# A long convolution in six channel parts inside the first feed-forward units, with the feed-forward width in thirds

## The chip, the cores and the metric

The kernel runs on one core of a Trainium2 chip. The metric is the time of one execution on the device in microseconds (us); less is better. A profile is one further execution, recorded by the hardware: it lists what each engine did and when. The engines are PE (matrix products), PEld (loads of its weights, which overlap them), DVE (vector operations), ACT (activations), POOL (a general vector engine that here also issues the loads of x) and SP, which here only issues transfers. Transfers run on 16 DMA engines.

## The reference

Two layers, each of a gated convolution (A) and a gated feed-forward (B), on x of 2048 tokens by 576 channels. The convolution has the same inputs k, v, ssm_k in both layers, so its y is the same in both.

```python
def _A_ref(q, k, v, shift_k, ssm_k, ssm_D):
    # k_shift: causal filter of 4 taps along the tokens
    kv = k_shift * v
    y = irfft(rfft(kv, 2S) * rfft(ssm_k, 2S))[:S]     # causal convolution of length S = 2048
    return q * (y + kv * ssm_D)

def _B_ref(x, w_gate, w_up, w_down):                  # 576 -> 4608 -> 576
    return (_gelu(x @ w_gate) * (x @ w_up)) @ w_down

x = A_q
for _ in range(2):
    x = x + _A_ref(_layernorm(x), ...)
    x = x + _B_ref(_layernorm(x), ...)
```

## The kernel before

**The convolution** (`ssm_conv`) works on four blocks of 512 tokens. A block of kv or of the filter h is turned into a spectrum of 1024 rows by matmuls with a matrix GF (`fwd`, L125 to L132: for each of 8 row tiles four matmuls, then ACT copies PSUM to SBUF). GF and the inverse matrix GI are made on the chip: DVE makes integer phases (L55, L59), ACT takes their sine (L60). For block m, DVE multiplies spectra K of block a with H of block m - a (L219), PE sums the products in PSUM by matmuls with an identity (L223), ACT copies the sum to Y (L229), DVE adds the Y of the block before with a sign, which makes Z (L233, L236), and PE brings it back with GI (L242), from where ACT copies it into y_sb (L244). The 576 channels go in two parts, of 512 and of 64. kv is made in eight groups of 256 tokens: four shifted loads of k and one of v, all double-buffered, then eight DVE operations (L178 to L183).

All of the convolution stands ahead of the feed-forward. Only the loads of x for chunk 0, its gate and its normalisation, and the first three weight groups are put in after block 0 (`on_block`, L390).

**The feed-forward** goes in eight units, a unit being one layer of one chunk of 512 tokens: (0,0), (0,1), (1,0), (0,2), (1,1), (0,3), (1,2), (1,3) as (layer, chunk). A unit has a gate/up phase and a down phase. In gate/up, for each of 36 tiles f of 128 features, 18 matmuls (L438) with K of 64 rows fill two PSUM banks, ACT applies the gelu to one (L441) and DVE multiplies by the other into hT (L442); four pairs of banks are used in turn. Weights of w_gate and w_up arrive in groups of three f (wgu, three buffers, L298 to L301, rows of 768 bytes). In the down phase, for each of four rows j of 128 tokens, 36 pairs of matmuls of 512 and 64 columns (L458, L459) sum over f; DVE adds x (L466, L467). w_down (wd) is loaded once, in unit 0, and stays (L430).

The next unit's gate (`gate_steps`: mean and variance, POOL's power for 1/sigma at L329, two DVE operations) and normalisation (`ln_steps`) are DVE steps that are taken one by one after each f (L443); then eight transposing transfers (`spread`, L358) make xnT, the moving operand of the next gate/up phase. These are issued after the gate/up phase, so that the down phase lies beside them. After layer 0's down phase the gate of layer 1 follows at once (L471).

A scheduler of the framework decides the order of instructions on each engine, by dependences and program order. Transfers issued by SP go out in SP's order.

Of the kernel before, what the change touches and what calls it, by code (L numbers as in the profile page):

```python
# [11 lines left out]
ALU = mybir.AluOpType  # L12
# [11 lines left out]
def _gen_dft_mats(tc, pool_gf, pool_gi, G_dtype):  # L24
    nc = tc.nc
    N4 = 4 * NDFT
    KT_F = BS // P
    KT_I = NDFT // P
    GF = pool_gf.tile([P, KT_F, NDFT], G_dtype, name="GF")
    GI = pool_gi.tile([P, KT_I, BS], G_dtype, name="GI")  # L30
    with ExitStack() as es:
        tmpc = es.enter_context(tc.tile_pool(name="dft_tmp", bufs=1))
        work = es.enter_context(tc.tile_pool(name="dft_work", bufs=2))
        rowv = tmpc.tile([P, KT_F], F32, name="rowv")
        nc.gpsimd.iota(rowv[:], pattern=[[2 * P, KT_F]], base=1, channel_multiplier=2,
                       allow_small_or_imprecise_dtypes=True)
        rowf = tmpc.tile([P, 2, KT_F], F32, name="rowf")
        nc.gpsimd.iota(rowf[:], pattern=[[0, 2], [2 * P, KT_F]], base=1, channel_multiplier=2,
                       allow_small_or_imprecise_dtypes=True)
        colf = tmpc.tile([P, NF], F32, name="colf")  # L40
        nc.gpsimd.iota(colf[:], pattern=[[2, NF]], base=1, channel_multiplier=0,
                       allow_small_or_imprecise_dtypes=True)
        colt = tmpc.tile([P, BS], F32, name="colt")
        nc.gpsimd.iota(colt[:], pattern=[[2, BS]], base=2, channel_multiplier=0,
                       allow_small_or_imprecise_dtypes=True)
        negpi = tmpc.tile([P, 1], F32, name="negpi")
        nc.vector.memset(negpi[:], -math.pi)
        sc = 2.0 * math.pi / N4

        def emit(dst, col_ap_halves, row_scalar, offs):  # L50
            W = sum(w for _, w in col_ap_halves)
            j = work.tile([P, NDFT], I32, tag="dft_j", bufs=1)
            c0 = 0
            for (cap, w), off in zip(col_ap_halves, offs):
                nc.vector.tensor_scalar(out=j[:, c0:c0 + w], in0=cap, scalar1=row_scalar,  # L55
                                        scalar2=float(off), op0=ALU.mult, op1=ALU.add)
                c0 += w
            jm = work.tile([P, NDFT], I32, tag="dft_jm")
            nc.vector.tensor_single_scalar(out=jm[:, 0:W], in_=j[:, 0:W], scalar=N4 - 1, op=ALU.bitwise_and)  # L59
            nc.scalar.activation(out=dst, in_=jm[:, 0:W], func=ACT.Sin, bias=negpi[:], scale=sc)  # L60

        for kt in range(KT_F):
            emit(GF[:, kt, :], [(colf[:], NF), (colf[:], NF)], rowv[:, kt:kt + 1],
                 [3 * NDFT, 0])
        for kt in range(KT_I):
            off = 3 * NDFT if kt < KT_F else 0
            emit(GI[:, kt, :], [(colt[:], BS)], rowf[:, kt // KT_F, kt % KT_F: kt % KT_F + 1], [off])
    return GF, GI

@with_exitstack
def ssm_conv(ctx, tc, y_sb, ident, A_k, A_v, A_shift_k, A_ssm_k, A_ssm_D, on_block):
    nc = tc.nc
    G_dtype = BF16
    k2 = A_k[0]
    v2 = A_v[0]
    S, D = k2.shape
    NST = S // P
    NBLK = S // BS  # L80
    STB = BS // P
    KT_F = BS // P
    KT_I = NDFT // P
    MT = NDFT // P
    HM = MT // 2
    KS = A_shift_k.shape[1]
    parts = []
    o = 0
    while o < D:
        w = min(512, D - o)  # L90
        parts.append((o, w))
        o += w

    fpool = ctx.enter_context(tc.tile_pool(name="A_freq", bufs=1))
    gip = ctx.enter_context(tc.tile_pool(name="A_gi", bufs=1))
    psT = ctx.enter_context(tc.tile_pool(name="A_psT", bufs=4, space=PSUM))
    psY = ctx.enter_context(tc.tile_pool(name="A_psY", bufs=2, space=PSUM))

    kv_es = ExitStack()
    gfp = kv_es.enter_context(tc.tile_pool(name="A_gf", bufs=1))  # L100
    kvp = kv_es.enter_context(tc.tile_pool(name="A_kv", bufs=2))
    dvec = gfp.tile([1, D], BF16, name="dvec")
    nc.sync.dma_start(out=dvec[:], in_=A_ssm_D.unsqueeze(0))

    def load_h(blk):
        hT = kvp.tile([P, STB, D], BF16, tag="blk", name=f"hT{blk}")
        nc.sync.dma_start_transpose(out=hT[:], in_=A_ssm_k[:, blk * BS:(blk + 1) * BS])
        return hT

    hT_next = load_h(0)  # L110
    GF, GI = _gen_dft_mats(tc, gfp, gip, G_dtype)
    kc = kv_es.enter_context(tc.tile_pool(name="A_kc", bufs=1))
    ktmp = kv_es.enter_context(tc.tile_pool(name="A_ktmp", bufs=2))
    sgn_i = gip.tile([P, 1], I32, name="sgn_i")
    nc.gpsimd.iota(sgn_i[:], pattern=[[0, 1]], base=0, channel_multiplier=1)
    sgn_b = gip.tile([P, 1], I32, name="sgn_b")
# [406 lines left out]
```

## Time and profile before

Three runs took 1095.11, 1095.13 and 1094.2 us: median 1095.11. The profiled execution took 1096.94 us, with a span of 1095.2 us from its first to its last instruction.

| engine | busy us | share of the span | instructions |
|---|---|---|---|
| PE | 1014.3 | 93% | 8433 |
| PEld | 488.2 | 45% | 8496 |
| DVE | 499.2 | 46% | 1024 |
| ACT | 256.3 | 23% | 486 |
| POOL | 56.8 | 5% | 79 |

The page moves 122.81 MB in all, 112 GB/s over the span. A share of busy time is a mean over stages that differ: one has to ask which stage has which limit, and which wait ends last there. PE's 93% also counts matmuls whose ends are modelled and which overlap, so it does not say how near PE is to its own limit; the start-to-start distances on PE's timeline do.

### The profile page before, as it was taken

Reading aid. Unit: us, or ns where it says so; the run is one execution under the profiler, and the core shown is the slowest. Engines: PE = TensorE matmul, PEld = TensorE weight load, DVE = VectorE, ACT = ScalarE, POOL = GpSimd, SP = SyncE. Lnnn points to the kernel's source line nnn. Section 1 sums busy time; section 2 is a strip of 40 time slices with the busy share of each in tenths; the row PEclk is TensorE's granted clock in tenths of the full one; section 3 lists DMA queues with packets and bytes.
Section 4 is the critical chain, followed back from the end, with each engine's and each line's share of the span. In section 5 each row is a group of like instructions: output and inputs, shape, how many; then the busy total and the mean of one; then the engine's idle time right before and its main releaser. Section 6 shows DMA issues by size and latency. Waiting matters only on the chain.

```text
span 1095.2 us, 19986 instructions
## 1 busy us (share of the span) xinstructions
PE 1014.3 (93%) x8433; PEld 488.2 (45%) x8496; DVE 499.2 (46%) x1024; ACT 256.3 (23%) x486; POOL 56.8 (5%) x79
## 2 busy tenths in 40 slices
PE   4887688869999999799999997999999999999998
PEld 1343233425554445355544453555444544454444
DVE  6396689673355323943123338432233553203320
ACT  5565232113202320133023201330132023202310
POOL 2000100020010001300000012000000100000000
PEclk9899889989999999999999999999999999999999
DMA  9881100297734772377457733674377347725710
GB/s 183 197 268 33 27 18 1 63 289 154 145 66 95 151 139 51 66 145 150 91 129 149 149 58 66 130 160 90 77 160 143 67 96 150 141 65 120 147 38 17
DMA packets 183802, 122.81 MB, mean 112 GB/s; under 512 B 54053, under 2 KB 181536, under 8 KB 183712
## 3 DMA queue, kind: packets, MB, share of 16 engines
q1 hardware_dynamic: 181600, 116.81, 51.3%
q0 software_dynamic: 2112, 4.72, 1.5%
q8 instruction: 66, 1.08, 0.4%
q14 instruction: 24, 0.20, 0.1%
HBM read 104.98 MB, written 2.36 MB: 98 GB/s over the span
## 4 chain that ended last, share of the span: by engine, by line
PE 79%; DVE 13%; issue 3%; DMA 2%; POOL 1%; ACT 1%; SPq 0%; DVEq 0%; POOLq 0%
PE ps L438 47%; PE ps L458 22%; PE ps L459 4%; PE ps L129 3%; DVE pr L219 3%; DVE stats L321 2%; PE ps L242 2%; PE Yps L223 2%; POOL rstd L329 1%; DVE acc L182 1%; DVE tmp L181 1%; DVE hT L442 1%; DVE g_t L338 1%; DMA x_c<-in_A_q_dram 1%; DMA kj<-in_A_k_dram 1%
## 5 line engine op out<-in xcount | busy, mean ns | idle before, releaser
L438 PE MATMUL ps<-xnT,wgu 64*128 64x512 bf16 x5184 | 571.7, 380 | 24.2 <-DVE hT L442 23.8
L438 PEld LDWEIGHTS <-wgu 64*128 64x128 bf16 x5184 | 267.5, 95 | 326.3 <-issue 40.1
L442 DVE TENSOR_TENSOR hT<-ga,ps 128x512 bf16<-128x512 f32 x288 | 197.1, 687 | 316.8 <-ACT ga L441 316.2
L441 ACT ACTIVATE ga<-ps 128x512 f32<-128x512 f32 x288 | 172.1, 597 | 667.8 <-PE ps L438 599.5
L458 PE MATMUL ps<-wd,hT 128*128 128x512 bf16 x1104 | 278.1, 380 | 0.0
L459 PE MATMUL ps<-wd,hT 128*128 128x64 bf16 x1152 | 222.0, 193 | 2.5
L458 PEld LDWEIGHTS <-hT 128*128 128x128 bf16 x1152 | 112.7, 98 | 139.4 <-issue 3.4
L459 PEld LDWEIGHTS <-hT 128*128 128x128 bf16 x1152 | 112.9, 98 | 0.0
L329 POOL TENSOR_TENSOR rstd<-ve,neghalf_t 128x1 f32<-128x1 f32 x64 | 51.6, 807 | 666.4 <-DVE ve L328 654.9
L219 DVE TENSOR_TENSOR pr<-KVf,Hf 128x1024 bf16<-128x1024 bf16 (+1 forms) x160 | 62.1, 450 | 22.4 <-PE Yps L223 13.3
L129 PEld LDWEIGHTS <-GF 128*128 128x128 bf16 x512 | 35.5, 102 | 68.8 <-issue 24.2
L129 PE MATMUL ps<-hT,GF 128*128 128x512 bf16 (+1 forms) x253 | 40.7, 318 | 20.2 <-ACT GF L60 13.6
L466 DVE TENSOR_TENSOR ob<-x_c,ps 128x512 bf16<-128x512 f32 x16 | 11.0, 687 | 103.8 <-PE ps L459 103.8
L321 DVE BATCH_NORM_STATS2 stats<-x_c 128x6 f32<-128x288 f32 x128 | 52.6, 441 | 9.9 <-DMA x_c<-in_A_q_dram 9.6
L223 PE MATMUL Yps<-pr,ident 128*128 128x512 bf16 (+1 forms) x175 | 45.8, 341 | 8.0 <-DVE pr L219 6.0
L242 PE MATMUL ps<-zb,GI 128*128 128x512 bf16 (+1 forms) x189 | 35.6, 301 | 10.7 <-DVE zb L233 6.6
L466 DVE TENSOR_TENSOR x_c<-x_c,ps 128x512 f32<-128x512 f32 x16 | 11.0, 688 | 70.8 <-PE ps L459 70.8
L129 PE MATMUL ps<-kv,GF 128*128 128x64 bf16 (+1 forms) x252 | 34.5, 292 | 9.2 <-DVE kv L183 7.7
L242 PEld LDWEIGHTS <-GI 128*128 128x128 bf16 x256 | 19.6, 100 | 30.9 <-issue 16.8
L352 DVE TENSOR_SCALAR xn<-x_c,mv,rstd 128x576 bf16<-128x576 f32 x32 | 18.5, 579 | 29.1 <-DMA xnT<-xn 16.7
L223 PEld LDWEIGHTS <-ident 128*128 128x128 bf16 x180 | 17.6, 100 | 28.0 <-issue 15.3
L342 DVE SCALAR_TENSOR_TENSOR x_c<-g_t,rstd,x_c 128x576 f32<-128x576 f32 x32 | 26.1, 815 | 6.9 <-POOL rstd L329 6.9
(48 smaller groups left out, 272.8 us busy)
## 6 DMA issues: line engine op xcount, KB each, us to landing
wgu<-in_B_w_gate_dram SPq DMA_DIRECT2D x96, 432.0 KB, 4.8
wgu<-in_B_w_up_dram SPq DMA_DIRECT2D x96, 384.0 KB, 6.1
kj<-in_A_k_dram SPq DMA_DIRECT2D x29, 288.0 KB, 4.6
wd<-in_B_w_down_dram SPq DMA_DIRECT2D x12, 432.0 KB, 11.5
x_c<-in_A_q_dram POOLq DMA_DIRECT2D x4, 1152.0 KB, 8.3
wgu<-in_B_w_up_dram SPq DMA_DIRECT2D x96, 48.0 KB, 5.5
v_t<-in_A_v_dram SPq DMA_DIRECT2D x8, 288.0 KB, 3.6
out_dram<-ob SPq DMA_DIRECT2D x16, 144.0 KB, 1.8
```

Source lines behind the costliest of these rows:

```text
L129: nc.tensor.matmul(ps[:], lhsT=GF[:, kt, mt * P:(mt + 1) * P], rhs=src_blk[:, kt, d0:d0 + dw], start=(kt == 0), stop=(kt == KT_F - 1))
L219: nc.vector.tensor_tensor(out=pr[:], in0=kvf[:, ko:ko + HH, :], in1=hf[:, ho:ho + HH, :], op=ALU.mult)
L223: nc.tensor.matmul(Yflat[:, c0:c0 + cw], lhsT=idm[:], rhs=prf[:, c0:c0 + cw], start=(ti == 0), stop=(ti == n_terms - 1))
L242: nc.tensor.matmul(ps[:], lhsT=GI[:, kt, mt * P:(mt + 1) * P], rhs=zb[:, kt, :], start=(kt == 0), stop=(kt == KT_I - 1))
L321: nc.vector.bn_stats(out=v["st"][:, h, :], in_=xa[:, h * hw:(h + 1) * hw])
L329: nc.gpsimd.tensor_tensor(out=v["rstd"][:], in0=ve[:], in1=neghalf_t[:, 0:1], op=ALU.pow)
L342: nc.vector.scalar_tensor_tensor(out=xa, in0=v["t"][:], scalar=v["rstd"][:, 0:1], in1=xa, op0=ALU.mult, op1=ALU.add)
L438: nc.tensor.matmul(pd[:], lhsT=w[r0:r0 + HK, k, fi * P:(fi + 1) * P], rhs=xnT[r0:r0 + HK, b, :], start=(k == 0), stop=(k == NKC - 1))
L441: nc.scalar.activation(out=ga[:], in_=pg[:], func=ACT.Gelu_apprx_tanh)
L442: nc.vector.tensor_tensor(out=hT[:, f, :], in0=ga[:], in1=pu[:], op=ALU.mult)
L458: nc.tensor.matmul(am[:], lhsT=lh, rhs=d[:, f % FG, 0:DM], start=(f == 0), stop=(f == FT - 1))
L459: nc.tensor.matmul(ar[:], lhsT=lh, rhs=d[:, f % FG, DM:D], start=(f == 0), stop=(f == FT - 1))
```

## The change

The convolution is cut into six parts of 96 channels. Only block 0 of all parts, and six filter spectra of parts 0 and 1, stand ahead of the feed-forward; the rest is a list of small steps (`Filler`) that are put between the matmuls of units 0 and 1. The order of the units is now (0,0), (1,0), (0,1), (0,2), (1,1), (0,3), (1,2), (1,3). A unit is three times a third: 12 f of gate/up, then a down phase over these 12 f for all four rows j, with an addition to x each time. Weights of w_gate and w_up come in groups of two f (three buffers, rows of 512 bytes), and w_down is loaded anew in each third, six transfers, six buffers. The order on every engine is the order in which the kernel's text names the instructions (`manual_schedule`). POOL makes the phases of GI. k and v are single-buffered.

```diff
+class Dft:
+    def inverse(self, kt):
+        off = 3 * NDFT if kt < self.KT_F else 0
+        self._sin(self.nc.gpsimd, self.GI[:, kt, :], self.colt, BS,
+                  self.rowf[:, kt // self.KT_F, kt % self.KT_F: kt % self.KT_F + 1], [off], "i")
...
+class Conv:
+    PW = 96
+    def spectrum(self, what, p, blk, src, c0):
...
+            ps = self.bank(HM * PW)
+            for i in range(HM):
+                mt = h * HM + i
+                for kt in range(self.dft.KT_F):
+                    nc.tensor.matmul(ps[:, i * PW:(i + 1) * PW], lhsT=self.dft.GF[:, kt, mt * P:(mt + 1) * P],
+                                     rhs=src[:, kt, c0:c0 + PW], start=(kt == 0), stop=(kt == self.dft.KT_F - 1))
...
+        return [lambda: half(0), lambda: half(1)]
+    def product(self, p, m):
...
+    def inverse(self, p, m):
...
+        return [lambda: part(0), lambda: part(1)]
...
+class Filler:
...
+    def term(self):
...
+    def step(self):
...
+    FG = 2
+    SUB = 3
+    FS = FT // SUB
+    GS = FS // FG
...
+    units = [(0, 0), (1, 0), (0, 1), (0, 2), (1, 1), (0, 3), (1, 2), (1, 3)]
+    ctx.enter_context(tc.manual_schedule())
...
+    wpool = left("wgu", 3)
+    dpool = left("wd", GS)
...
+    prp = right("A_prod", 6)
...
+    cvp = right("A_cv", 1)
...
+    nc.sync.dma_start(out=skb[:].rearrange("p d j -> p (d j)"),
+                      in_=A_shift_k.rearrange("d j -> (d j)").partition_broadcast(P))
+    dvec = tmp.tile([1, D], BF16, name="dvec")
+    nc.sync.dma_start(out=dvec[:], in_=A_ssm_D.unsqueeze(0))
+    load_kv(0, nc.sync)
+    hT0 = kvt.tile([P, BS // P, D], BF16, name="hT0", tag="blk")
+    nc.sync.dma_start_transpose(out=hT0[:], in_=A_ssm_k[:, 0:BS])
...
+        def begin():
+            if g not in shifts:
+                load_kv(g, nc.sync)
...
+    for _ in range(2 * len(early)):
+        fill.step()
+    for _ in range(GS):
+        load_d()
...
+    for g in range(2, NST // GST):
+        vec.extend(kv_steps(g))
...
     for ui, (layer, c) in enumerate(units):
...
+        for sub in range(SUB):
+            end = sub == SUB - 1
...
+            for f in range(FS):
...
+                b0 = 2 * ((f + 2) % 4)
...
+                if f % FG == FG - 1:
+                    load_w()
+                if prep:
+                    prep.popleft()()
+                    if prep and f % 2:
+                        prep.popleft()()
+                else:
+                    vec_step(1 if f % 2 else 2)
+                    fill.prefetch(DEPTH, 1)
+            if end and nxt is not None and not same and xn_next and not prep and len(xn_next) == STC:
+                xnT_next = new_xnT(ui + 1)
+                for j in range(STC):
+                    spread(xnT_next, j, xn_next[j])
+
+            ds = [d_in.popleft() for _ in range(GS)]
+            for n in range(9):
+                if not fill.step():
+                    break
+                fill.prefetch(DEPTH)
...
             for j in range(STC):
+                am = bank(2 * (j % 2), DM)
+                ar = bank(2 * (j % 2) + 1, DR)
+                for f in range(FS):
...
+                    if f == 2 and resid:
+                        resid.popleft()()
+                    if fill.term():
+                        fill.flush(3)
+                    else:
+                        fill.flush(0)
+                        fill.step()
+                    fill.prefetch(DEPTH)
+                    if f % 2 and not fill.ahead:
+                        vec_step(1)
+                        if prep:
+                            prep.popleft()()
...
+            for _ in range(GS):
+                load_d()
+        if nxt is not None and not same and xnT_next is None:
...
+            while prep:
+                prep.popleft()()
+            xnT_next = new_xnT(ui + 1)
+            for j in range(STC):
+                spread(xnT_next, j, xn_next[j])
```

Of the new functions: `Dft.inverse` has POOL make the phases of a GI tile, DVE mask them and ACT take the sine. `spectrum` and `inverse` each give two steps of 16 matmuls of 96 columns, with an ACT copy out of PSUM. `product` gives terms: a DVE product of 384 columns, its identity matmul and, after the last of a sum, the copy to Y and the making of Z. `fill.prefetch` issues DVE products ahead, `fill.term` one identity matmul, `fill.step` one step of a spectrum or an inverse whose needs are made. `load_w` loads one group of w_gate and w_up, `load_d` two f of w_down. `resid` holds the additions to x of the row before and, at a unit's end, the gate, and the normalisation and `spread` too if the next unit has the same chunk. `begin` is the first DVE step of a kv group, and issues that group's loads.

In the last lines `same` means that the next unit has the same chunk (unit 0 to unit 1), `end` that this is a unit's last third, and `prep` holds the steps of the next unit's gate and normalisation; they are taken up at the start of a third if x is loaded and, for layer 0, all six parts of y are done.

## The prediction

> **What bounds the kernel now.** I read the cores view first (one core, span 1095.2 us, granted clock 0.975), then the chain of waits in order of time, which cuts the span into stages, then busy time by stage, and last PE's, SP's and DVE's own timelines.
>
> From the chain, in time order (start, length, what):
>
> ```profile
> 1.15 7.53 DMA hT<-in_A_ssm_k_dram
> ...
> 213.53 8.38 DMA x_c<-in_A_q_dram
> ...
> 333.14 70.04 PE ps L438 x648
> ...
> 880.63 70.04 PE ps L438 x648
> 986.06 70.04 PE ps L438 x648
> ```
>
> From unit 6 to unit 7 is 986.06 - 880.63 = 105.43 us: 70.04 of gate/up and 35.4 of down, without a gap. Eight units are 843.4. PE's timeline has the first gate/up matmul at 213.4, so the span is 213.4 convolution + 843.4 + 34.7 lost inside units + 3.7 tail (last matmul 1091.5). The chain puts the 34.7 in unit 0 (14.3: unit 1 starts 119.7 after it), unit 2 and unit 4 (10 each: 554.17 and 775.21 come late).
>
> By stage (length, busy PE, PEld, DVE, ACT, POOL with counts, granted clock, DMA share, GB/s):
>
> ```profile
> 105.00:213.00 108.00, 87.40 (x488) 39.99 (x496) 90.03 (x216) 25.50 (x55) 4.08 (x4) 0.91 0.06 12
> ...
> 213.00:244.00 31.00, 21.54 (x163) 9.95 (x163) 19.70 (x54) 5.78 (x11) 7.54 (x10) 0.87 1.12 300
> ...
> 333.00:403.00 70.00, 70.00 (x650) 31.45 (x648) 29.19 (x49) 20.90 (x35) 1.60 (x2) 1.00 0.70 140
> 403.00:438.60 35.60, 35.29 (x286) 18.24 (x292) 11.26 (x26) 0.60 (x1) 2.96 (x3) 1.00 0.32 60
> ```
>
> The feed-forward is PE's alone; the convolution is a relay of DVE, PE and ACT. Within 105-213 DMA does nothing, and in 213-244 DMA is full and PE waits for DVE.
>
> **The change, part by part.**
>
> *Convolution matmuls.* In the built order of the changed program, 768 matmuls of 96 columns (576 spectra, 192 inverses) and 24 of 384 stand ahead of unit 0; 1536 of 96 and 216 of 384 stand in units 0 and 1; none later. Their price comes from two stretches of PE's timeline:
>
> ```profile
> 59.96 0.87 PE L129 MATMUL ps<-hT,GF 128*128 128x64 bf16 x20 [0.34 <-ACT Hf L132]
> ```
>
> ```profile
> 116.43 0.22 PE L223 MATMUL Yps<-pr,ident 128*128 128x128 bf16 x1
> ```
>
> Twenty 64-wide ones take 0.87, that is (0.87 - 0.19)/19 = 36 ns from start to start, each with its own weights; the 128-wide ones start at 116.43, 116.48, 116.54 and 116.59, 53 ns apart. 96 lies between: 0.0425 us. 384 columns go by the down pair, whose 512 + 64 columns take 0.2457: 0.163. Woven work: 1536 x 0.0425 + 216 x 0.163 = 65 + 35 = **100 us**, all on PE, which is already full there. So the weave does not hide it; it only fills what idle time PE would have. (The Trainium skill, "TensorE: Matmul & The Clock Gate", section "Back-to-back issue gap", gives some 81 ns for a sustained 128-wide matmul with its weight load; by that the 1536 would cost 124 us, 59 more. The 53 ns of this trace speak against it.)
>
> *Ahead of unit 0* (213.4 before). DVE's order is now fixed. The four GF steps no longer stand behind hT: 2 + 6.6 us (9.3 to 15.9 in the trace) = 9. hT0 is queued on SP behind skb and the first k and v loads, some 2 MB: I take 14 for its landing (7.5 alone). dvec, signs and skc 2.3; first kv group 8 x 0.79 = 6.3, to 22.8; the second has the same single buffers, so its loads start as the first is read: 29. Then eight jm each wait for a POOL operation that was DVE's. No row has it: DVE's own is 0.48, POOL's IOTA of that size 0.56, its AFFINE_SELECT of 128 columns 0.28, times four 1.13. I take 0.8 (nearest the IOTA, with two operations): 8 x (0.8 + 0.42) = 10, to 39; by the ends 36 to 42. Statistics 3.9, to 43. ACT's K evictions stand behind the eight sines (40), done 45; products 24 x 0.25, to 49 (0.25 is worked out below); inverses 192 x 0.0425 = 8.2, to 58. Four gate-and-normalise rows in series, each 0.73 x 2 + 1 + POOL 1.06 + 0.6 = 4.2: 75. SP's last transposes 77.5, then three small H transposes which PE's order wants before unit 0: **85** (80 to 95: POOL's ends, hT0 at 12 or 17, and a clock of 0.5 on the 8 us of inverses).
>
> *Unit 0: k and v.* Six kv groups are now woven in, with single buffers, their loads issued by SP at the point where DVE wants the data. So DVE waits a whole landing (4.7 for kj), and behind the waiting DVE instruction stand the hT products that free PSUM: PE can go four or five f ahead (9.7 us), as in 213-244, where the same kind of wait cost 14.3. At the start SP also has six wd (1.77 MB), k and v (1.47 MB) and a wgu group. Rates when DMA is full (share over 1): 203 GB/s with wgu alone, 386 with wd:
>
> ```profile
> 18.00:20.00 2.00, 2.00 (x6) 0.75 (x5) 2.00 (x8) 2.00 (x5) 0.75 (x1) 1.00 1.14 203
> ...
> 217.00:221.00 4.00, 4.00 (x41) 2.13 (x38) 0.00 (x0) 1.03 (x2) 0.00 (x0) 1.00 1.34 386
> ...
> 237.00:241.00 4.00, 1.82 (x10) 0.61 (x8) 3.01 (x7) 0.60 (x1) 1.71 (x2) 0.50 1.10 271
> ```
>
> wd 4.7, k 4, wgu 3: the fourth group lands at 14.5 instead of 11.7, and the third kv group holds hT f=11 until about 33 where the down phase wants it at 28; then groups 4 and 5 run at load pace, 54 for a third whose PE work is 42. Loss 12, 3 in the next third, 2 for the lower clock (0.50 in the last line, amid such waits): **17** (3 if every landing fits in the 9.7; 28 for six whole landings of 4.7).
>
> *Unit 0 to 1.* Unit 1 is the same rows, so the gate, normalisation and transposes of row j stand between DVE's products. A product of 384 columns is 0.25 (eleven of 1024 take 5.31, four of 128 take 0.63), a Z 0.55 (1.28 and 0.34). Last third: 36 x 0.25 + 6 x 0.55 + 4 x (0.82 of addition + 2.8 of gate + 2.7 of normalisation, a POOL wait of 1.1 in each) = 37 on DVE against 33 on PE, then two transposes and their landing 4, less the spectra that PE has left, of which I let half (2.4 of 4.8) count, and 3 of stalls inside: **9** (3 to 15: all of the spectra and no stall; none of them and twice the stall). Other relay stalls (term after product, inverse after Z, DVE in order): 36 Z hand-overs at some 0.2: **8** (2 at 0.05, 20 at a whole Z of 0.55).
>
> *Unit 1 to 2.* Unit 2's preparation starts only in unit 1's last third, 28 steps where the gate/up loop takes 18. So the transposes stand on SP behind the outputs (1.5) and six wd (4.5): 1.5 + 4.5 + 12.2 = **18** (16 to 21.5, as a wd issue takes 0.37 or, in a full queue, 1.3), the 12.2 from SP's timeline, as eight take 10.97 and the last lands 2.5 after its issue:
>
> ```profile
> 845.31 10.97 SPq L362 DMA_TRANSPOSE xnT<-xn  x8
> ```
>
> *The five other unit ends.* These transposes follow the last wgu issue (2.0) and end 14.1 after gate/up. 35.4 of down hid that; a third hides 11.8: 2.3 each, **11.5** (6 with the shortest issue of 1.19; 20 with the longest landing of 4.3).
>
> *Unit 4.* x of the last chunk is issued on POOL after unit 3's last rstd and lands 8.3 later; the statistics that wait for it stand ahead of hT f=1: **7** (3 to 11: PE stalls alone, or the longest landing of x, 12.2). Unit 2's x lands inside the 18.
>
> *Streaming.* 37 MB of wd more, and wgu rows of 512 bytes where 768 were. In a gate/up stretch:
>
> ```profile
> q1 hardware_dynamic: 12000, 8.85, 74.4%
> ```
>
> 59 us x 16 x 0.744/12000 = 58.5 ns a packet. A group keeps 1152 packets; by packets it takes 4.2 us as now, by bytes 2.9. A group may take two groups' time, 7.8 us, and now lands 6.7 after its issue (0.6 + 0.65 + 5.5), so I cost streaming at nothing; the cover is 1.1 us. (The Trainium skill, "DMA: Bandwidth & Descriptors", section "Specifications", has 512 bytes and above at line rate, about 27 GiB/s an engine; by that a group is some 1.3 us. Here 768-byte rows reached 200 GB/s, less than half of it.) The extra residual adds, 64 x 0.9 = 58 us, lie on DVE under PE's down phases.
>
> *Sum of the span:* 85 + 843.4 + 100 + 17 + 9 + 8 + 18 + 11.5 + 7 + 3.7 = 1102.6. The profiled execution took 1096.94 against its span of 1095.2 and the median of 1095.11, so a span stands for a median here. Forecast **1103**, 0.7% slower: the front and woven work are 185 where 213.4 were, 28 gained, and the losses grow from 34.7 to 70.5.
>
> **Rivals.**
>
> *DVE is not held (faster).* k and v land before DVE wants them, because SP runs ahead of PE further than I give it. Place: the six kv groups of unit 0. It decides if k lands within the four to five f (9.7 us) that PSUM holds each time. Then 17 goes to 3, the relay 8 to 2, unit 0 to 1 from 9 to 6: 1103 - 23 = 1080; with the low ends of front and unit ends (10.5 more) 1069. For it: in 59-95 of the trace DVE ran kv groups at 6.15 each without loss, but with double buffers; against it: single ones here.
>
> *The wgu stream becomes the bound (slower still).* If 512-byte packets keep 58.5 ns, a third needs 6 x 4.2 + 1536 wd rows x 58.5 ns/16 = 31 of its 35.1 us; one landing over 7.8 and PE waits. 1 us at two groups of each of 18 thirds is 36, and unit 0 10 more: 1103 + 46 = 1149. For it: landings of wgu in 213-245 were 9.4 to 12.5 when wd ran beside it. Against: there the queue also had x.
>
> That the weave does not happen is excluded by the built order.
>
> **How the numbers follow.** Forecast as summed (1093 to 1130) 0.47; DVE not held (1066 to 1093) 0.36; stream bound (1130 to 1160) 0.17. Range 1066 to 1150 leaves out some 0.15. Runs of this kernel tell about 0.2% (2.2 us) from no change: faster 0.36, same 0.05, slower 0.59.
>
> **What would show it.** Right: unit 0's gate/up starts near 85; DVE waits for DMA k_sh in unit 0 and PE for hT; a gap of some 18 before unit 2 with SP in transposes and gaps of 2 to 3 at later unit ends; three thirds without loss at 105.4; 96-wide matmuls 40 to 45 ns apart. Wrong: a front over 95 or under 75 (POOL, hT0), PE waiting for wgu in the middle of units 5 to 7 (the stream), units 0 and 1 together under 320 (DVE not held).

## The result and the profile after

The changed kernel takes 1161.6 us (median of four runs, 1156.0 to 1165.0), the kernel before 1095.1 beside it: ratio 1.0603, with a 95% interval of 1.0561 to 1.0646. It is 6% slower, where 0.7% was forecast and 5% was the upper end of the range. The profiled run took 1164.98 us, with a span of 1163.2 and a granted clock of 0.956 (0.975 before).

What PE waited for in the changed kernel (waiting line, releaser: us in total, times, longest):

```profile
PE ps L738 <- DMA xnT<-xn: 25.5, 9, 18.4
PE ps L114 <- DVE sgn_b L534: 22.9, 1, 22.9
PE ps L114 <- DMA hs<-in_A_ssm_k_dram: 21.1, 2, 19.4
PE ps L142 <- DVE pr L136: 15.8, 5, 5.0
...
PE ps L770 <- DVE x_c L792: 7.6, 2, 3.9
```

L738 is the gate/up matmul, L770 the down matmul, L114 a spectrum, L142 the sum of products. The two lines of L114 belong to the front: the 22.9 is the time up to PE's first matmul, and 19.4 of the other is a wait for a transfer of the filter (hs) just before unit 0. Behind the front no line explains the loss: it is spread over many places. By stage (the columns are those of the prediction's table): the front, the three thirds of unit 0, and a third of unit 3:

```profile
0.00:95.83 95.83, 45.80 (x792) 40.53 (x793) 50.79 (x120) 36.33 (x66) 13.14 (x28) 0.86 0.46 95
95.83:162.72 66.89, 49.99 (x427) 24.90 (x430) 40.79 (x74) 12.78 (x22) 0.00 (x0) 0.90 0.88 207
162.72:219.00 56.28, 54.02 (x586) 31.16 (x590) 40.27 (x95) 14.90 (x28) 0.00 (x0) 1.00 0.55 129
219.00:303.90 84.90, 68.00 (x839) 45.46 (x845) 45.27 (x113) 21.88 (x42) 7.14 (x9) 0.91 0.36 81
636.10:671.40 35.30, 35.20 (x314) 16.48 (x315) 11.52 (x20) 7.16 (x12) 0.00 (x0) 1.00 0.60 150
```

The chain of waits shows the undisturbed third and three of the transfers that something waits for:

```profile
12.93 9.40 DMA hT<-in_A_ssm_k_dram
...
481.06 2.50 DMA xnT<-xn
...
636.17 23.42 PE ps L738 x216
...
671.46 23.42 PE ps L738 x216
...
833.42 7.80 DMA wgu<-in_B_w_up_dram
```

From 636.17 to 671.46 is a third: 23.42 of gate/up and 11.87 of down, 35.3, and three make 105.8 where a unit before took 105.4. The feed-forward itself lost 0.4 a unit. Everything else against the prediction's sum:

| stage | forecast (us) | measured (us) |
|---|---|---|
| front, to the first gate/up matmul | 85 | 95.8 |
| eight units, undisturbed | 843.4 | 846.7 |
| woven work | 100 | 100 (prices as forecast: 42.5 ns and 0.164 us start to start) |
| losses in units 0 and 1 | 17 + 9 + 8 + 18 = 52 | 75: first third 24.3, second 3.0, last 22.7, unit 1's 2.6, 3.5 and 18.5 |
| losses in units 2 to 7 | 11.5 + 7 = 18.5 | 41.9 |
| tail | 3.7 | 3.7 |
| span | 1102.6 | 1163.2 |

Measured losses are the distances from one first gate/up matmul to the next, less the work at these prices. The 41.9 is the sum of 10.0, 4.6, 11.0, 7.5, 3.9 and 4.9 for units 2 to 7; the middle and last gate/up phases of all six are 23.4.

### The profile page after: what moved, and what is told of

Its sections match the earlier page's. It is cut to its first block, busy times and chain, and to the rows that moved or that the text cites. A ratio compares the mean times of both kernels' runs of the same rounds, so it can differ in the third digit from the quotient of the medians.

```text
span 1163.2 us, 23752 instructions
## 1 busy us (share of the span) xinstructions
PE 1022.0 (88%) x9966; PEld 541.8 (47%) x10032; DVE 566.2 (49%) x1236; ACT 259.7 (22%) x458; POOL 56.4 (5%) x87
## 3 DMA queue, kind: packets, MB, share of 16 engines
HBM read 142.14 MB, written 2.36 MB: 124 GB/s over the span
## 4 chain that ended last, share of the span: by engine, by line
PE 72%; DVE 11%; DMA 7%; SPq 4%; issue 3%; POOL 2%; ACT 0%; DVEq 0%; POOLq 0%
PE ps L738 44%; PE ps L770 15%; PE ps L142 4%; PE ps L114 3%; PE ps L771 3%; PE ps L186 3%; SPq L520 2%; DMA wgu<-in_B_w_up_dram 2%; DVE stats L479 2%; POOL rstd L487 2%; DMA k_sh<-in_A_k_dram 2%; DVE x_c L500 1%; DMA xnT<-xn 1%; DVE ks_tmp L457 1%; DVE acc L460 1%
## 5 line engine op out<-in xcount | busy, mean ns | idle before, releaser
L738 PE MATMUL ps<-xnT,wgu 64*128 64x512 bf16 x5184 | 581.1, 382 | 51.1 <-DMA xnT<-xn 25.5
L738 PEld LDWEIGHTS <-wgu 64*128 64x128 bf16 x5184 | 264.0, 95 | 362.3 <-issue 65.2
L770 PE MATMUL ps<-wd,hT 128*128 128x512 bf16 x1086 | 310.3, 387 | 7.6 <-DVE x_c L792 7.6
L770 PEld LDWEIGHTS <-hT 128*128 128x128 bf16 x1152 | 114.0, 99 | 131.3 <-issue 27.4
L792 DVE TENSOR_TENSOR x_c<-x_c,ps 128x512 f32<-128x512 f32 x80 | 54.8, 685 | 96.9 <-PE ps L771 96.9
L114 PEld LDWEIGHTS <-GF 128*128 128x128 bf16 x1536 | 73.4, 103 | 60.0 <-issue 36.6
L142 PE MATMUL ps<-pr,ident 128*128 128x384 bf16 x180 | 60.8, 344 | 15.8 <-DVE pr L136 15.8
L114 PE MATMUL ps<-kv,GF 128*128 128x96 bf16 x768 | 40.1, 214 | 11.6 <-DVE kv L463 9.6
L114 PE MATMUL ps<-hs,GF 128*128 128x96 bf16 x576 | 29.8, 214 | 21.1 <-DMA hs<-in_A_ssm_k_dram 21.1
L186 PEld LDWEIGHTS <-GI 128*128 128x128 bf16 x768 | 35.2, 99 | 6.7 <-issue 4.0
L186 PE MATMUL ps<-Zb,GI 128*128 128x96 bf16 x576 | 30.4, 209 | 2.4 <-DVE Zb L164 2.4
L136 DVE TENSOR_TENSOR pr<-Ks,H 128x384 bf16<-128x384 bf16 x72 | 23.8, 353 | 17.3 <-PE ps L142 12.3
L142 PEld LDWEIGHTS <-ident 128*128 128x128 bf16 x180 | 17.8, 102 | 27.1 <-DVE pr L136 4.9
L496 DVE SCALAR_TENSOR_TENSOR g_t<-x_c,mv,y_sb 128x576 f32<-128x576 f32 x32 | 25.9, 809 | 9.1 <-ACT y_sb L190 9.1
L114 PE MATMUL ps<-hT,GF 128*128 128x96 bf16 x192 | 9.7, 220 | 22.9 <-DVE sgn_b L534 22.9
```

The source lines that it names most:

```text
L114: nc.tensor.matmul(ps[:, i * PW:(i + 1) * PW], lhsT=self.dft.GF[:, kt, mt * P:(mt + 1) * P], rhs=src[:, kt, c0:c0 + PW], start=(kt == 0), ...
L142: nc.tensor.matmul(v["ps"][:], lhsT=idm[:], rhs=w["pr"][:].rearrange("p a b -> p (a b)"), start=(i == 0), stop=(i == n - 1))
L186: nc.tensor.matmul(ps[:, mt * PW:(mt + 1) * PW], lhsT=self.dft.GI[:, kt, mt * P:(mt + 1) * P], rhs=self.Z[(p, m)][:, kt, :], start=(kt == ...
L738: nc.tensor.matmul(pd[:], lhsT=w[r0:r0 + HK, k, fi * P:(fi + 1) * P], rhs=xnT[r0:r0 + HK, b, :], start=(k == 0), stop=(k == NKC - 1))
L770: nc.tensor.matmul(am[:], lhsT=lh, rhs=d[:, f % FG, 0:DM], start=(f == 0), stop=(f == FS - 1))
L792: nc.vector.tensor_tensor(out=dst[:, 0:DM], in0=xa[:, 0:DM], in1=am[:], op=ALU.add)
```

## The experiments

Theory 1: the missing 60 us are many separate waits, each made by the order of one in-order engine or queue (DVE, SP, POOL), with a lower clock behind each gap. Theory 2, a family of rivals: the weave or the streamed weights cost rate, so a wait that is removed comes back elsewhere. Each ratio is to runs of the kernel before on the same chip, with its 95% interval; "after" has 1.0603. Profiles of kernels that leave unit 0 as it is start unit 1 anywhere between 297.5 and 303.9, so totals that differ by some 5 us prove little by themselves, and I read the edited stage.

**The unit ends, units 2 to 7.** Transposes earlier:

```diff
-            if end and nxt is not None and not same and xn_next and not prep and len(xn_next) == STC:
+            if ((end or ui >= 2 and len(xts) == 2) and xnT_next is None and nxt is not None and not same
+                    and xn_next and not prep and len(xn_next) == STC):
```

> The transposes of a unit's successor go out one or two thirds earlier in units 2 to 7, as soon as its normalised rows are there. Theory 1 (a transfer that no longer hides behind a short down phase, plus the low clock after the gap): the five gaps of 1.9 to 3.1 us go (12 us), the 2.1 to 2.5 us of lower clock after three of them go too (7), and the outputs no longer stand behind transposes on SP, which may give up to 8 in units 5 and 7: 1161.6 falls by 19 to 27, to 1135-1143; first-third gate/up of units 3 and 6 comes to 23.4-24. Rival A (the gap alone, the clock is low for another reason): falls by 12, to 1150, and these gate/up phases stay at 25.5-25.9. Rival B (the time is given back because wd and wgu now stand behind the transposes in the middle thirds): within 4 us of 1161.6, with PE waiting for wgu or wd there.

Measured: 1158.2, ratio 1.0578 (1.0527 to 1.0628). Both theories were right in part. The gaps went and so did the slow matmuls behind them: first gate/up phases of units 3, 5, 6 and 7 at 23.4, 25.1, 23.5 and 24.0 (25.9, 29.1, 25.5 and 28.3), all last down phases 11.87. That is 22 us, within theory 1's figure. But 21 were lost again, most of it in thirds that had lost nothing (+3.4, +1.5, +5.0, +0.9, +1.6 in gate/up, +1.7 in down, +7.2 at unit 4). From 470 on, PE waited eleven times for wgu:

```profile
PE ps L738 <- DMA wgu<-in_B_w_up_dram: 4.9, 7, 1.1
PE ps L738 <- DMA wgu<-in_B_w_gate_dram: 4.2, 4, 2.1
```

So eight transposes in one piece cost about the same in whichever third they are issued; by SP's order, it reaches wd and then wgu too late behind them. The next kernel issues one behind each wgu group:

```diff
                 if f % FG == FG - 1:
                     load_w()
+                    if tq:
+                        tq.popleft()()
```

> In units 2 to 7 the eight transposes of the next unit go out in a later third than the one that made the rows, one behind each wgu group of its gate/up phase and three behind the last. Early transposes in one piece had removed the gaps (first gate/up of units 3 and 6 at 23.4) but added waits for wgu in the third they were moved to (up to 7 us). Theory 1 (they held the queue ahead of wgu): here the gaps go and no such wait comes, the time falls by 18 to 24, to about 1140. Rival (a transpose slows the wgu transfers beside it wherever it stands): PE waits for wgu in these thirds, 1153 or above.

Measured: 1150.6, ratio 1.0509 (1.0477 to 1.0541). The gaps went and middle thirds stayed at 23.4; what is left is unit 4's first gate/up (32.0, where other profiles have 26.6 to 29.9; see x below) and wgu in unit 5. The rival's "a transpose slows wgu wherever it stands" is out; theory 1's size was reached by half, and most of what is missing lies at unit 4.

Whether the clock is low because PE was idle:

```diff
+            if ui >= 3 and sub == 0:
+                pg = bank(4, CH)
+                for _ in range(10):
+                    nc.tensor.matmul(pg[:], lhsT=w_in[0][0:HK, 0, 0:P], rhs=old[0:HK, 0, :], start=True, stop=True)
```

> At the start of units 3 to 7, ten more matmuls of 512 columns (2.2 us) into a bank that is overwritten right after; their operands are there before the unit's end, so PE works while it waits for xnT. Theory 1 (idle time of 1.2 to 3 us is what lowers the granted clock after it): the first gate/up phases of units 3 and 6, measured from their first own matmul, go from 25.5-25.9 to 23.4-23.8, and the dummies take the place of the gap: the time falls by 3 to 6, to about 1157. Rival (the clock is low there for another reason, such as the transposes): the phases stay above 25 and the time rises by up to 4.

Measured: 1156.9, ratio 1.0565 (1.0536 to 1.0593). PE's timeline at unit 3 with the dummies (start, length; in brackets the idle time before):

```profile
591.89 2.33 PE L731 MATMUL ps<-xnT,wgu 64*128 64x512 bf16 x10
594.27 0.39 PE L742 MATMUL ps<-xnT,wgu 64*128 64x512 bf16 x2
595.24 5.12 PE L742 MATMUL ps<-xnT,wgu 64*128 64x512 bf16 x45 [0.58 <-issue]
```

Its windows there, the last but two number being the granted clock:

```profile
592.00:594.00 2.00, 2.00 (x10) 0.75 (x8) 1.71 (x5) 0.00 (x0) 0.81 (x1) 1.00 0.46 90
596.00:598.00 2.00, 2.00 (x22) 1.03 (x19) 1.64 (x5) 0.60 (x1) 0.87 (x1) 1.00 1.03 339
```

And the changed kernel at the same place, after idle times of 2.36 and 0.71:

```profile
598.40:600.40 2.00, 1.28 (x8) 0.52 (x10) 2.00 (x5) 0.00 (x0) 0.00 (x0) 0.72 0.63 166
600.40:602.40 2.00, 2.00 (x13) 0.75 (x11) 1.49 (x5) 0.00 (x0) 0.99 (x1) 0.50 1.01 305
```

That is 13 matmuls in 2 us at 0.50 against 22 at 1.00. From the first own matmul, unit 3's phase is 24.2 where it was 25.9, above theory 1's 23.8. One pair of profiles would not show a cause, as a gap does not always bring the low clock. In the twelve profiles that keep the gaps before units 3 to 7 (0.9 to 2.9 us), the clock fell to 0.50 within 2.5 us of the unit's first matmul at 28 of the 60 starts. In the seven without the gaps (this one, and those with the transposes moved) it did so at none of 35. So the idle time is the cause, though not by its length alone. Here is such a start in a run below (that without preparation in the down phases); the last line is the window behind:

```profile
807.93 0.39 PE L738 MATMUL ps<-xnT,wgu 64*128 64x512 bf16 x2 [1.21 <-issue]
809.11 3.29 PE L738 MATMUL ps<-xnT,wgu 64*128 64x512 bf16 x18 [0.79 <-DMA xnT<-xn]
809.90:813.30 3.40, 3.40 (x20) 1.50 (x16) 2.25 (x6) 0.60 (x1) 0.00 (x0) 0.50 0.34 102
```

A stretch of 3.4 us at 0.50 costs 1.7 us of work. At unit 7 of the run with outputs by POOL, idle times of 2.33 and 1.11 left the clock at 1.00 for the 12 us behind. (The Trainium skill, "TensorE: Matmul & The Clock Gate", "What's actually happening", says the half clock comes after at least one idle window of about 3.4 us. Here idle times of 1.2 and 0.8 us were enough in the first of these cases, and 2.3 and 1.1 were not in the second.)

The next three edits are for outputs, x, and preparation in the down phase. Outputs issued by POOL:

```diff
-                        nc.sync.dma_start(out=out2[st * P:(st + 1) * P, :], in_=ob[:])
+                        nc.gpsimd.dma_start(out=out2[st * P:(st + 1) * P, :], in_=ob[:])
```

(with four buffers for ob)

> Outputs are issued by POOL instead of SP, and have four buffers. Theory 1 (wgu of the next unit stands on SP behind outputs that wait for DVE): the first gate/up of units 5 and 7 falls from 29.1 and 28.3 (26.2 to 31 in other profiles) to 25-26, as in unit 6, unit 2's transposes start 1.5 earlier; the time falls by 4 to 8, to about 1156. Rival (six wd ahead of wgu are the cause, in every third; here the gap only uncovers it): both stay above 27, with PE waiting for wgu.

Measured: 1153.0, ratio 1.0523 (1.05 to 1.0546). Unit 5's first gate/up phase is 23.7 and unit 7's 24.7, and the wait before unit 2 went from 18.9 to 14.4. After 800 PE waits for no wgu at all:

```profile
PE ps L738 <- DMA xnT<-xn: 7.4, 5, 2.3
```

Outputs ahead of wd and wgu on SP were the cause. The edit has two parts, though, the queue and the buffers, and no run separates them. In the changed kernel the third output at the end of unit 4 waits on DVE for a buffer, as the first two outputs stand on SP behind the eight transposes; here DVE has no such wait:

```profile
827.55 0.69 DVE L792 TENSOR_TENSOR ob<-x_c,ps 128x512 bf16<-128x512 f32 x1 [8.22 <-DMA out_dram<-ob]
```

x of the last chunk earlier:

```diff
+            if ui == 3 and sub == 0:
+                load_x(NCH - 1)
```

> x of the last chunk is loaded at the start of unit 3 instead of unit 4. Theory 1 (the statistics that wait for it stand on DVE ahead of the hT that PE wants): the first gate/up of unit 4 (26.6 to 28.5 us so far) falls to 24-25.5, the time by 2 to 4, to 1158, little, because the 28 preparation steps then run into the same down phase. Rival (the low clock after the gap is all of it): it stays above 26 and the time does not move.

Measured: 1156.1, ratio 1.0552 (1.0526 to 1.0578). Unit 4's first gate/up is 24.3 (26.6 to 29.9 with the late load), as theory 1 had it; its down phase stays at 18.6.

No preparation step in the down phases from unit 2 on:

```diff
-                        if prep:
+                        if prep and ui < 2:
                             prep.popleft()()
```

> From unit 2 on no preparation step of the next unit is taken in a down phase, so the residual additions that free PSUM stand on DVE behind none of them. Theory 1: the first down phases of units 2 and 4 fall from 17.1 and 18.4 us to 12, the time by 11 to 1150. Rival (these down phases wait for wd or for hT, not for the additions): they stay at 17-18 and the time within 3 us of 1161.6.

Measured: 1147.4, ratio 1.0462 (1.0412 to 1.0511). The first down phases of units 2 and 4 went from 17.1 and 18.4 to 11.9 and 12.7, 10.8 in all, as theory 1 had it: the next unit's steps stood on DVE ahead of the additions that free PSUM.

**Unit 1 to 2.** Unit 2's preparation taken faster in unit 1's last third:

```diff
-                    prep.popleft()()
-                    if prep and f % 2:
-                        prep.popleft()()
+                    for _ in range(2 + (f % 3 == 0) if ui == 1 else 1 + f % 2):
+                        if prep:
+                            prep.popleft()()
```

> In the last third of unit 1 the 28 preparation steps of unit 2 are taken at 2.33 per f instead of 1.5, so its eight transposes go out before the down phase and not behind the outputs and six wd. Theory 1: the 18.4 us wait for xnT before unit 2 becomes some 2.5, the time falls by 16 to about 1146. Rival (DVE is full in that third, so the steps hold hT): the third's gate/up grows from 23.4 to 28 or more and at most 8 are gained, 1153 or above.

Measured: 1146.8, ratio 1.0451 (1.0424 to 1.0478). Unit 1's last third is 51.2 where it was 63.1; the wait for xnT is gone (18.9 before; 1.4 for wgu comes in its place), and the third's gate/up is 26.3 as before. This is theory 1, with 4.5 of new waits and 3.4 us at half the clock in the down phase, so that the third gave 11.9; what the total fell beyond that is not in the edited stage.

**Unit 0: rate or order.** k and v loaded a group ahead:

```diff
+            if g + 1 < NST // GST:
+                load_tap(g + 1, i)
```

> Each k and v load of the next kv group is issued as soon as DVE has read the same buffer for this group, a group's length ahead of its use; no buffer is added. Theory 1 (a landing on DVE's path, with hT behind it): the waits of DVE for k_sh of 6.3, 5.4 and 3.8 us go, the first third of unit 0 falls from 66.9 to 50-53 us, the time by 14 to some 1147. Rival (the first third is short of DMA rate: 10 MB in it): it stays above 60 us, the waits move to wgu or wd, and at most 5 are gained.

Measured: 1157.8, ratio 1.0564 (1.0541 to 1.0588); the first third is 59.3, between the expectations. DVE's waits for k_sh shrank to one of 1.6, yet 16.7 of loss remained (eight profiles with the old loads have 61.7 to 66.9 for this third). Two stretches of it:

```profile
105.00:115.00 10.00, 6.08 (x35) 2.01 (x33) 3.98 (x7) 1.12 (x3) 0.00 (x0) 0.72 1.16 212
115.00:125.00 10.00, 10.00 (x90) 4.29 (x87) 7.79 (x12) 2.85 (x5) 0.00 (x0) 0.94 1.12 223
```

The DMA share is over 1 (1.16, 1.12) at some 215 GB/s. So I took bytes away:

```diff
+        if 0 < i < KS:
+            shifts[g][0].append((j, shifts[g][0][0][1]))
-        if i < KS:
+        elif i < KS:
```

(the one tile of k that is left has two buffers)

> As the kernel with early k and v loads, but from kv group 1 on only one of the four shifted loads of k is made and used for all four taps; 2 loads a group instead of 5, so 864 KB less in each (the computed y is therefore another). That kernel's first third of unit 0 took 59.3 us with DMA full at 205 to 223 GB/s. Theory A (the transfer rate is the limit there): the third falls to 46-50 us, with DMA's share below 1 in most of it, and the time by 10 against that kernel, to 1147. Theory B (the waits come from DVE's order and the relay): it stays above 56 us.

Measured: 1149.1, ratio 1.0504 (1.0474 to 1.0534); the third is 55.9, between the two, though DMA's share is below 0.7 from 115 on:

```profile
115.00:125.00 10.00, 10.00 (x112) 5.11 (x109) 8.96 (x15) 3.48 (x6) 0.00 (x0) 1.00 0.65 144
125.00:135.00 10.00, 8.54 (x88) 5.21 (x87) 9.24 (x20) 1.96 (x4) 0.00 (x0) 1.00 0.46 115
```

So the issue of the loads and their rate make 6 to 11 of the loss. In these two rows DVE is busy for 0.9 of the time: its kv work, with the relay behind it, is what I take for the rest; that is argued and not shown.

Gate and normalisation steps between the products of unit 0's last down phase:

```diff
-                        for t in gate_steps(c, j):
-                            t()
                         if same:
-                            for t in ln_steps(c, j, xn_next):
-                                t()
+                            post.extend(gate_steps(c, j) + ln_steps(c, j, xn_next))
```

(post gives one step per f from f=3 on)

> In unit 0's last down phase the gate and normalisation steps of row j are taken one per f between the next row's products instead of in one piece. Theory 1 (a row's chain of 6.7 us holds the products that PE waits for): the last down phase of unit 0 falls from 54.4 (51.7 to 54.4 in five profiles) to 43-46, the time by 8 to 10, to about 1152. Rival (the products, Z and inverses in series are the limit, and the last row's chain stands in any case): the phase stays above 50 and the time within 4 us of 1161.6.

Measured: 1154.0, ratio 1.0551 (1.0519 to 1.0583). The down phase is 48.4, between the expectations: 3.3 to 6.3 of it was the row chain (51.7 to 54.7 in the profiles without this edit), and the last row's chain still stands.

**The front.** The filter's transfer and three of its spectra earlier:

```diff
-    load_kv(0, nc.sync)
     hT0 = kvt.tile([P, BS // P, D], BF16, name="hT0", tag="blk")
     nc.sync.dma_start_transpose(out=hT0[:], in_=A_ssm_k[:, 0:BS])
+    load_kv(0, nc.sync)
```

(and six steps of H spectra ahead of the inverses)

> The first filter block's transposing transfer goes out ahead of the first k and v loads, and three of the six early H spectra are taken ahead of block 0's inverses, so that three more small H transposes go out on SP before the eight of xnT. Theory 1 (SP's order sets the front): hT lands near 13 instead of 22.3, DVE's work behind it moves 5 to 8 earlier, and the 19.4 us wait for hs at 89.5 goes; unit 0's gate/up starts at 80 to 84 instead of 95.8, the time falls by 12 to 16, to about 1148. Rival (POOL's phases and the four gate and normalisation rows set the front): it starts at 88 or later, with PE waiting for xnT, and at most 8 are gained.

Measured: 1154.7, ratio 1.0554 (1.0516 to 1.0592). Unit 0 starts at 87.1, between the expectations. PE's first matmul comes at 14.0 where it came at 22.9, and the wait for hs is gone: SP's order was 9 of the front. In the changed kernel SP stood for 7.3 us at one of the k loads that were ahead of hT:

```profile
3.45 7.27 SPq L372 DMA_DIRECT2D k_sh<-in_A_k_dram  x1
```

The rival's wait for xnT, 17.0, is what comes next. In the chain of the kernel with five edits (below), which holds this one, DVE (jm) and POOL (j) take turns on the eight phases (30.52 to 39.59):

```profile
30.52 0.35 DVE jm L57
30.95 0.70 POOL j L54
...
39.15 0.44 DVE jm L57
```

The phases moved forward, in the changed kernel:

```diff
         dft.forward(kt)
+    for kt in range(dft.KT_I):
+        dft.inverse(kt)
```

(and not behind the kv groups)

> The eight phase steps of the inverse matrix (POOL 0.7, DVE 0.44 in series, 10 us) come right after those of the forward matrix, where DVE waits for hT and k, and no longer behind the two kv groups. Theory 1 (front as a relay on DVE): unit 0's gate/up starts 7 to 10 earlier, at 86-89, the time is 7 to 10 less, about 1153. Rival (hs behind the transposes of xnT on SP decides): products and rows come earlier and the start stays above 92.

Measured: 1151.9, ratio 1.0529 (1.0491 to 1.0567). Unit 0 starts at 90.0, 5.8 earlier, 1 short of theory 1's figure; PE still waits 19.3 for hs, so that the shift went through although SP's order stayed.

**The stream.** wd between the wgu groups:

```diff
                     load_w()
+                    if ui or sub:
+                        for _ in range((1, 2, 2, 1, 0, 0)[f // FG]):
+                            load_d()
```

(and not six behind the down phase)

> From the second third on, wd is issued one or two at a time behind the wgu groups of the gate/up phase and no longer six at once ahead of them, and the outputs have four buffers. Theory 1 (SP's order and the burst of wd make wgu late): the first gate/up of units 5 and 7 falls from 29.1 and 28.3 to some 25, the waits for wgu at the start of unit 0's thirds shrink, the time falls by 7 to 10, to about 1153. Rival (wgu's own rate is the limit): PE waits for wgu as before or for wd, within 4 us of 1161.6.

Measured: 1177.2, ratio 1.0761 (1.0724 to 1.0799): slower, which neither theory had. A wgu transfer took this long from issue to landing in the median (last number), first here, then in the changed kernel:

```profile
wgu<-in_B_w_gate_dram SPq DMA_DIRECT2D x144, 288.0 KB, 7.0
```

```profile
wgu<-in_B_w_gate_dram SPq DMA_DIRECT2D x144, 288.0 KB, 4.1
```

The prediction had worked out 6.7 landing against 7.8 of cover. With wd alongside, that cover is nearly used up and wd itself comes late (11 waits of PE, 8.6 us); six wd in a burst ahead of the phase cost less. Of the 12.7 us that this profile loses from unit 2 on, 5.0 lie in the middle thirds and 6.9 in the last ones, partly in longer gaps before the next unit (12.9 in all for 9.1); why those grew is open. This is the one run in which the stream binds, and the change does not go there.

**Sums**

The edits of the early k and v loads, the quicker preparation in unit 1, the down phases, the woven rows and the front's transfers together:

> Five edits together: quicker preparation in unit 1's last third, early k and v loads, no preparation steps in down phases from unit 2 on, hT and H spectra earlier in the front, gate steps woven into the products. Alone they took 14.8, 3.9, 14.2, 7.0 and 7.7 off 1161.6. Theory 1 (separate waits at separate places): they add up to 47.6, 1114. Rival (the three of unit 0 hide one another, a wait removed is waited for next): at most 36, 1125 or above.

Measured: 1120.1, ratio 1.0219 (1.0193 to 1.0244): 41.5 of 47.6. Most of it adds up.

Then with the transposes one by one and the rows of the front side by side:

> The five, and the transposes one behind each wgu group, and the four rows of the front's first gate and normalisation taken side by side instead of one after another. Theory 1: 12 to 20 less than the five for the unit ends and 4 to 6 for the front: 1090 to 1098, near the kernel before (1095). Rival: the transposes give the gain back in wgu waits and POOL's powers set the front: 1108 or above.

Measured: 1111.5, ratio 1.0143 (1.0119 to 1.0166): not the 1090 to 1098. The time is the rival's, but the places are not. Rows side by side (all four gates, then all statistics, then all four normalisations) finish together: SP's eight transposes start at 77.0 instead of 68.8, and unit 0 at 87.7 instead of 84.6. The unit ends lost nothing, but unit 4's first gate/up took 34.0. POOL issues x at 669.79, PE waits with DVE's hT behind the statistics that wait for it:

```profile
669.79 0.78 POOL L414 DMA_DIRECT2D x_c<-in_A_q_dram  x1
```

```profile
681.29 16.37 PE L770 MATMUL ps<-xnT,wgu 64*128 64x512 bf16 x125 [7.59 <-DVE hT L774]
```

Then without the rows side by side, and with early x, outputs by POOL and early phases, nine edits in all:

> The five (1120.1 against 1096.2), transposes one behind each wgu group, x of the last chunk early, outputs by POOL, phases early. Theory 1 (separate waits): 1120 less 9 to 10 for unit ends (as the gap's share of the seven-part version), 10 for unit 4's x (34.0 there), 5 for outputs and 8 for the phases: 1084 to 1092, below the kernel before by 0.5 to 1%. Rival (unit 0 takes up what the front gives): 1097 or above, with PE's waits in unit 0 grown by as much as the front shrank.

Measured: 1095.6 against 1096.2, ratio 0.9991 (0.997 to 1.0011), the same. Units 3 to 7 lose 1.3, 0.1, 0, 1.0 and 0.1. What was missed of the expectation is unit 2's first phase, 30.4, where x of chunk 2 now stands behind the outputs on POOL. So that load goes out earlier:

```diff
+            if ui == 1 and sub == 1 and closed["cv"]:
+                load_x(2)
```

> The nine parts and x of chunk 2 loaded in unit 1 only. Theory (DVE waited 9.2 us for it at the start of unit 2, with hT behind): unit 2's first gate/up falls from 30.4 to 24-26, the time by 5 to 7, to about 1090, 0.5% below the kernel before. Rival (the low clock after the gap is most of it): above 28, within 2 us of the nine parts.

Measured: 1092.9, ratio 0.9979 (0.9962 to 0.9997). Unit 2's phase is 23.4, 7 gained; but unit 1 started later by nearly as much: POOL issued both loads at once, beside unit 1's last transposes, and PE's idle time there went from 3.56 to 9.76. The last down phase of unit 0 is 55.6 here and 55.2 in the next kernel, which has the same early load, against 47.3 to 48.8 in the four with woven rows and without it. So the early load costs this; that it delays the transposes' landing is my reading.

```profile
273.34 1.58 POOL L414 DMA_DIRECT2D x_c<-in_A_q_dram  x2 [0.26 <-issue]
```

```profile
286.99 5.24 PE L773 MATMUL ps<-xnT,wgu 64*128 64x512 bf16 x34 [9.76 <-issue]
```

And two kv groups moved into the front:

```diff
+    for g in (2, 3):
+        for t in kv_steps(g):
+            t()
```

(before the front's four rows, with the early x)

> The nine parts, and kv groups 2 and 3 made on DVE in the front, in the 13 us in which it waited for block 0's inverses (in the nine-part profile from 48 to 61), with their loads where DMA is little used; x of chunk 2 is loaded in unit 1. Theory (rate of transfer and DVE's order bound unit 0's first third): it falls from 63.8 us to 50-54, the front stays at 81.6 to 84, unit 2's first gate/up falls from 30.4 to 26 or less: 15 less than the nine parts (1095.6 against 1096.2), about 1080. Rival (the products and Z of the weave hold that third whatever DVE has to do for kv): it stays above 59, and 5 to 7 are gained by x alone, 1089 or above.

Measured: 1089.5 against 1095.8, ratio 0.995 (0.993 to 0.997): 0.5% faster than the kernel before, the best of the study. The first third is 58.1 and the second 52.5, where the nine parts had 63.8 and 57.5, and the front 85.8 for 81.6: against the kernel with x alone unit 1 starts 4.8 earlier, and the time is 3.4 less. The third lies between the two expectations, the time at the rival's.

## Why the prediction was wrong

*The sign* was right, and so was most of the sum's skeleton: woven work at 100, thirds without loss, 18 before unit 2 (18.5), 8 for the relay (6.1 in unit 1 alone; unit 0's part is not to be told from its other losses), 3 for the second third. The 18 has luck in it: SP's last output went out 2.8 after the down phase, not 1.5, and six wd took 3.1, not 4.5. Four terms were too small.

- *"The five other unit ends ... 2.3 each, 11.5", and "Unit 4 ... 7".* The gaps came as worked out (1.2 to 3.1 us). Put at nothing in the sum: the low clock after them (with short further waits 2.1 to 2.5 each in the first gate/up of units 2, 3 and 6), preparation steps that stand ahead of the additions in the down phase (5.2 and 6.5; without them, 10.8 came back), and outputs on SP ahead of wd and wgu (5.4 and 3.6 in the run with outputs on POOL). I had written that the additions "lie on DVE under PE's down phases"; they free PSUM, and what stands ahead of them counts. This is the largest error, 23.
- *"Unit 0 to 1 ... 9"* was 22.7. I counted DVE's work and not a row's chain of 6.7 in one piece between products that PE wanted; weaving the rows took 3.3 to 6.3 back. The rest of this term is not settled; I take it for products, Z, inverses and the last row in series.
- *"Front ... 85"* was 95.8. hT landed at 22.3, not 14, as SP stood for 7.3 us at one of the first k loads and issued hT only at 12.9 (why it stood there is not shown); and the three small H transposes I named became a wait of 19.4, for six stood behind xnT. POOL's 0.8 for a phase was near (0.70).
- *"Unit 0: k and v ... 17"* was 27.3. DVE did wait for landings (6.3, 5.4, 3.8), as forecast, and the 9.7 us that PE can go ahead did not cover them: in the first third PE waited 5.1 for kv, 4.4 for products, 3.3 for hT and 2.9 for wgu. The sum had put 12 on the pace of the loads; the two experiments there give their issue and rate 6 to 11. With most of these loads left out, some 13 of loss stay in this third (55.9 against 42.6 of PE's work); part of the relay's 8 belongs to them, the rest the sum did not have, and I take it for DVE's own work. The 386 GB/s that the sum used for wd was measured while a load of x was under way too (POOL issued two at 213.53).

The rival "DVE is not held" (0.36) was wrong in all its places. The rival "the wgu stream becomes the bound" reached nearest in time, for the wrong reason: the undisturbed third shows no wait. In a gate/up stretch of it (637 to 659) a packet took 22 us x 16 x 0.685/6510 = 37.0 ns, where 58.5 were feared:

```profile
q1 hardware_dynamic: 6510, 3.82, 68.5%
```

Its price set the range's upper end, so the range failed with the forecast: it held the sizes of known waits, and nothing for waits that were not on the list.

## What to carry to other kernels

Where every engine's order is fixed by hand, list for each engine what stands ahead of the instruction that frees a buffer the bottleneck wants, and for each queue what stands ahead of the transfer it wants; each gap that this leaves costs its length and, at about half of the unit starts here, 1.7 us of lower clock. A change that trades one long idle stage for many short hand-overs should be given a loss for each hand-over, and a range that is open towards more of them. And removing such waits one by one mostly paid here: nine edits that gave 82 us one by one gave 66 together, and with two more the 66 us came back, and 6 besides, by edits that leave the arithmetic as it is.

## What the runs showed of the hardware

- Idle times of PE of 0.9 to 2.9 us at a unit's start brought the clock to 0.50 at 28 of 60 starts, for 3.4 us at a time; at 35 starts without them, dummy matmuls included, it stayed at 1.00. Gap length alone did not decide it: 1.2 and 0.8 us did it in one profile, 2.3 and 1.1 did not in another.
- With k rows of 1152 bytes and wgu rows of 512 mixed, DMA at a share over 1 moved 205 to 223 GB/s (105 to 135 in the run with early k and v loads), near the 203 of wgu alone in rows of 768 before.
- A wgu transfer's landing went from 4.1 to 7.0 us when wd was issued between the groups, and with an x load of 1.2 MB more beside the transposes PE's idle time before the matmuls that wait for them grew by 6 (3.56 to 9.76).
